# Dilated attention followed by soft MoE: a mask built by doubling, and the MoE expert stages and their PSUM banks in another order

## The chip, the cores and the metric

The kernel runs on one core of one Trainium2 chip. Such a core has TensorE (PE in the profile; its weight loads are listed apart as PEld), VectorE (DVE), ScalarE (ACT), GpSimd (POOL), SyncE (SP) and 16 DMA engines. The metric is the device time of one execution in microseconds (us); lower is better. Times are compared as medians over several executions.

## The reference, cut to what matters

The first half is causal sliding attention over 8 batches, 8 heads, 576 positions and head dimension 64. Heads 0 to 3 use a plain window of 32 keys; heads 4 to 7 a dilated one, every fourth key out of 128. The result, as 4608 tokens of 512 features, goes through a soft mixture of experts with 8 experts of 4 slots each.

```python
mask_plain = (rel >= 0) & (rel < window)                                   # window = 32
mask_dil = (rel >= 0) & (rel < window * dilation) & (rel % dilation == 0)  # dilation = 4
...
logits = x @ phi                                   # 4608 x 32
d = np.exp(logits - logits.max(0, keepdims=True))
d /= d.sum(0, keepdims=True) + 1e-09
slot_input = (d.T @ x).reshape(E, S_per_e, D)      # 8 experts, 4 slots, 512
for e in range(E):
    h = np.maximum(slot_input[e] @ w1[e], 0.0)     # 4 x 1024
    slot_out[e] = h @ w2[e]                        # 4 x 512
c = np.exp(logits - logits.max(1, keepdims=True))
c /= c.sum(1, keepdims=True) + 1e-09
return c @ slot_out.reshape(n_slots, D)            # 4608 x 512
```

## The kernel before

The program is written out by hand. Each `@blk.<engine>` block appends instructions to that engine's queue, and every engine works through its own queue in order. `WT` makes an engine wait for semaphore counts, `SIG` raises one. A `Slot` remembers who wrote a buffer (`ready`) and who read it (`reads`); `war()` is the list that a new writer has to wait for.

**Setup (L199 to L258).** POOL builds an identity matrix and an index ramp, and fetches `phi`. DVE clears the eight PSUM banks and builds four 0/1 mask tiles in bf16, two for the plain window and two for the dilated one. The dilated pattern is a 128 x 256 band: the identity is added 32 times into `mtmp2`, each time 4 columns further right (L246 to L250), and every addition waits for the one before. Five copies (L251 to L257) then fill `mask_dA` and `mask_dB`.

**Attention (L324 to L539).** There are 32 units, one for each batch and pair of heads, in a software pipeline: load (`st_dmas`), cast of q on DVE (`st_qcast`), transposes on PE, evacuation on ACT, scores, exponentials on ACT, masking on DVE, the product with V (`st_pv`), normalisation into `x_sb`. q comes through SP's queue, three units ahead at most; k and v come through POOL's queue with a cast from f32 to bf16 on the way, and with every fourth unit 1 MB of `w1` (bf16) comes too. The first cast of q stands behind the masks on DVE.

**Slot inputs (L629 to L742).** x is transposed in groups of four tiles, the logits are computed and exponentiated, transposed to `e_tok` (tokens by slots), and `e_tok` times x is accumulated in `psF`. L769 scales the sum by the column sums, four transposes and a copy (L779, L788) give `siT`.

**Experts (L793 to L890).** `m6_stageA(e)` multiplies `siT` by `w1` in two halves of four matmuls (L806), ACT applies relu to each half (L817), PE transposes the result in eight small pieces (L830), DVE copies them to `hT` (L840). `m6_stageB(e)` multiplies `hT` by `w2` in eight matmuls (L855), ACT copies the 4 x 512 result to `so4` (L870), PE transposes it in four pieces (L879). The loop emits A of one expert, then B of the expert before. `w2` lives in a ring of three buffers; B(e) also lets POOL issue the load for e+3 (L618). The banks: A uses `psA`, `psB` for even and `psC`, `psD` for odd experts, B uses `psE` and `psF` in turn, the transposes of A use `psG`, those of B `psH`.

**Combine weights (L895 to L950).** After the last expert, L895, L905 and L914 turn the slot outputs into `so_slots`. Then DVE sums `e_tok` over the slots, inverts and scales it (L921, L924, L926) to `c_tok`, and nine rounds of four PE transposes into `psG` (L939) and one DVE copy (L948) give `cT`.

**Output (L952 to L996).** 36 tiles of 128 x 512: one matmul each from `cT` and `so_slots` (L961) into six banks in turn, copied by ACT or DVE to one of six staging buffers (L972, L979), and written out by SP's, ACT's or POOL's queue (L988).

Of the kernel before, what the change touches and what calls it, by code (L numbers as in the profile page):

```python
# [6 lines left out]
AluOp = mybir.AluOpType  # L7
ACTF = mybir.ActivationFunctionType
F32 = mybir.dt.float32
BF16 = mybir.dt.bfloat16  # L10
# [4 lines left out]
E_EXP = 8  # L15
SLOTS_PER_E = 4
N_SLOTS = E_EXP * SLOTS_PER_E
FF = 1024
SCALE = 1.0 / (D ** 0.5)
N_TT = N_TOK // 128  # L20
# [90 lines left out]
def bass_dilated_sliding_attn__then__soft_moe_slots_kernel(  # L111
# [14 lines left out]
    WT = env.waits  # L126
    SIG = env.sig
# [6 lines left out]
    ident = A(nc.sbuf_tensor("ident", [128, 128], BF16))  # L134
# [3 lines left out]
    mask_dA = A(nc.sbuf_tensor("mask_dA", [128, 512], BF16))  # L138
    mask_dB = A(nc.sbuf_tensor("mask_dB", [128, 512], BF16))
# [11 lines left out]
    mtmp1 = AA(nc.sbuf_tensor("mtmp1", [128, 512], BF16))  # L151
    mtmp2 = AA(nc.sbuf_tensor("mtmp2", [128, 512], BF16))
# [23 lines left out]
    blk = A(nc.Block())  # L176
# [43 lines left out]
    @blk.vector  # L220
    def _(vv):
        ev = None
        for pb in ps_sc + ps_pv + [ps_ta, ps_tb]:
            ev = SIG(vv, vv.memset(pb[:], 0.0))
        for s_ in sl_sc + sl_pv + [sl_pta, sl_ptb2]:
            s_.written(ev)
        if _DBG_STAGE:
            SIG(vv, vv.memset(x_sb[:], 0.0))
        WT(vv, [ev_iota[0]])
        e2 = SIG(vv, vv.tensor_scalar(mtmp1[:, 0:192], mtmp0[:, 0:192], 287.0, None, op0=AluOp.is_le))  # L230
        e3 = SIG(vv, vv.tensor_scalar(mtmp2[:, 0:192], mtmp0[:, 0:192], 256.0, None, op0=AluOp.is_ge))
        WT(vv, [e2, e3])
        e4 = SIG(vv, vv.tensor_tensor(mtmp1[:, 0:192], mtmp1[:, 0:192], mtmp2[:, 0:192], AluOp.mult))
        e5 = SIG(vv, vv.memset(mask_plA[:], 0.0))
        e6 = SIG(vv, vv.memset(mask_plB[:], 0.0))
        WT(vv, [e4, e5, e6])
        SIG(vv, vv.tensor_copy(mask_plA[:, 0:160], mtmp1[:, 0:160]))
        SIG(vv, vv.tensor_copy(mask_plA[:, 256:416], mtmp1[:, 0:160]))
        SIG(vv, vv.tensor_copy(mask_plB[:, 0:160], mtmp1[:, 0:160]))
        SIG(vv, vv.tensor_copy(mask_plB[:, 256:416], mtmp1[:, 0:160]))  # L240
        evm = SIG(vv, vv.tensor_copy(mask_plB[0:64, 448:512], mtmp1[0:64, 0:64]))
        sl_mask_pl.written(evm)
        WT(vv, [evm] + sl_ident.ready)
        e8 = SIG(vv, vv.memset(mtmp2[:, 0:256], 0.0))
        WT(vv, [e8])
        for kk in range(32):  # L246
            ei = SIG(vv, vv.tensor_tensor(mtmp2[:, 4 * kk:4 * kk + 128],
                                          mtmp2[:, 4 * kk:4 * kk + 128],
                                          ident[:, :], AluOp.add))
            WT(vv, [ei])  # L250
        SIG(vv, vv.tensor_copy(mask_dA[:, 0:256], mtmp2[:, 0:256]))  # L251
        SIG(vv, vv.tensor_copy(mask_dA[:, 256:512], mtmp2[:, 0:256]))
        e13 = SIG(vv, vv.memset(mask_dB[:], 0.0))
        WT(vv, [e13])
        SIG(vv, vv.tensor_copy(mask_dB[:, 0:256], mtmp2[:, 0:256]))
        SIG(vv, vv.tensor_copy(mask_dB[:, 256:448], mtmp2[:, 0:192]))
        evm = SIG(vv, vv.tensor_copy(mask_dB[0:64, 448:512], mtmp2[0:64, 0:64]))  # L257
        sl_mask_dl.written(evm)  # L258

    units = [(b_, p_) for b_ in range(B) for p_ in range(4)]  # L260
# [303 lines left out]
    e_tok = MA(nc.sbuf_tensor("e_tok", [128, N_TT, N_SLOTS], BF16))  # L564
    c_tok = MA(nc.sbuf_tensor("c_tok", [128, N_TT, N_SLOTS], BF16))
# [16 lines left out]
    psA, psB, psC, psD = ps_sc  # L582
# [4 lines left out]
    sl_psG, sl_psH = sl_pta, sl_ptb2  # L587
    psA_bf = psA[:].bitcast(BF16)
    psB_bf = psB[:].bitcast(BF16)
    psD_bf = psD[:].bitcast(BF16)  # L590
    psE_bf = psE[:].bitcast(BF16)
    psF_bf = psF[:].bitcast(BF16)
# [197 lines left out]
        sl_psE.reads.append(ev)  # L790
        sl_siT.written(ev)

    hbank = [[(psA, sl_psA), (psB, sl_psB)], [(psC, sl_psC), (psD, sl_psD)]]  # L793
    sobank = [(psE, sl_psE), (psF, sl_psF)]

    def m6_stageA(e):
        ep = e % 2
        for hh in range(2):
            psX, slX = hbank[ep][hh]

            @blk.tensor
            def _(pe, e=e, hh=hh, psX=psX, slX=slX):
                WT(pe, sl_siT.ready + sl_w1.ready + slX.war())
                last = None
                for c in range(4):
                    last = pe.matmul(psX[0:SLOTS_PER_E, 0:512],  # L806
                                     siT[:, c, 4 * e:4 * e + 4],
                                     w1b[:, e, c, 512 * hh:512 * hh + 512],
                                     start=(c == 0), stop=(c == 3))
                ev = SIG(pe, last)  # L810
                slX.written(ev)
                sl_siT.reads.append(ev)

            @blk.scalar
            def _(ac, e=e, hh=hh, psX=psX, slX=slX, ep=ep):
                WT(ac, slX.ready + (sl_h[ep].war() if hh == 0 else []))
                ev = SIG(ac, ac.activation(h_sb[ep][0:SLOTS_PER_E, 512 * hh:512 * hh + 512],  # L817
                                           psX[0:SLOTS_PER_E, 0:512], ACTF.Relu))
                slX.reads.append(ev)
                if hh == 0:  # L820
                    sl_h[ep].written(ev)
                else:
                    sl_h[ep].ready.append(ev)

        @blk.tensor
        def _(pe, e=e, ep=ep):
            WT(pe, sl_h[ep].ready + sl_psG.war())
            last = None
            for cc in range(8):
                last = pe.transpose(psG_bf[:, 4 * cc:4 * cc + 4],  # L830
                                    h_sb[ep][0:SLOTS_PER_E, 128 * cc:128 * cc + 128],
                                    ident[0:SLOTS_PER_E, 0:SLOTS_PER_E])
            ev = SIG(pe, last)
            sl_psG.written(ev)
            sl_h[ep].reads.append(ev)

        @blk.vector
        def _(vv, e=e, ep=ep):
            WT(vv, sl_psG.ready + sl_hT[ep].war())
            ev = SIG(vv, vv.tensor_copy(hT[ep][:, :, :],  # L840
                                        psG_bf[:, 0:32].rearrange("p (c s) -> p c s", s=4)))
            sl_psG.reads.append(ev)
            sl_hT[ep].written(ev)

    def m6_stageB(e):
# [22 lines left out]
        def _(ac, e=e, psX=psX, slX=slX, ep=ep):  # L868
# [2 lines left out]
            slX.reads.append(ev)  # L871
            sl_so4[ep].written(ev)

        @blk.tensor
        def _(pe, e=e, ep=ep):
            WT(pe, sl_so4[ep].ready + sl_psH.war())
            last = None
            for fc in range(4):
                last = pe.transpose(psH_bf[:, 32 * fc + 4 * e:32 * fc + 4 * e + 4],  # L879
                                    so4[ep][0:SLOTS_PER_E, 128 * fc:128 * fc + 128],  # L880
                                    ident[0:SLOTS_PER_E, 0:SLOTS_PER_E])
            ev = SIG(pe, last)
            sl_so4[ep].reads.append(ev)
            sl_psH.ready = list(sl_psH.ready) + [ev]

    for step in range(E_EXP + 1):
        if step < E_EXP:
            m6_stageA(step)
        if 0 <= step - 1 < E_EXP:
            m6_stageB(step - 1)  # L890

    @blk.vector
    def _(vv):
# [18 lines left out]
    def _(vv):  # L912
# [1 line left out]
        ev = SIG(vv, vv.tensor_copy(so_slots[:, :], psE_bf[0:N_SLOTS, 0:512]))  # L914
        sl_psE.reads.append(ev)
        sl_sos.written(ev)

    @blk.vector
    def _(vv):
        WT(vv, sl_etok.ready)  # L920
        e1 = SIG(vv, vv.tensor_reduce(rsum_tok[:, :], e_tok[:, :, :],  # L921
                                      mybir.AxisListType.X, AluOp.add))
        WT(vv, [e1])
        e2 = SIG(vv, vv.reciprocal(rsum_tok[:, :], rsum_tok[:, :]))  # L924
        WT(vv, [e2])
        ev = SIG(vv, vv.tensor_tensor(c_tok[:, :, :], e_tok[:, :, :],  # L926
                                      rsum_tok[:, :].unsqueeze(2).to_broadcast([128, N_TT, N_SLOTS]),
                                      AluOp.mult))
        sl_etok.reads.append(ev)
        sl_ctok.written(ev)  # L930

    for r in range(N_TT // 4):
        @blk.tensor
        def _(pe, r=r):
            WT(pe, sl_ctok.ready + sl_psG.war())
            last = None
            for ti in range(4):
                t = 4 * r + ti
                last = pe.transpose(psG_bf[0:N_SLOTS, 128 * ti:128 * ti + 128],  # L939
                                    c_tok[:, t, :], ident[:, :])  # L940
            ev = SIG(pe, last)
            sl_psG.written(ev)
            sl_ctok.reads.append(ev)

        @blk.vector
        def _(vv, r=r):
            WT(vv, sl_psG.ready + sl_cT.war())
            ev = SIG(vv, vv.tensor_copy(cT[:, 512 * r:512 * r + 512], psG_bf[0:N_SLOTS, 0:512]))  # L948
            sl_psG.reads.append(ev)
            sl_cT.written(ev)  # L950

    obank = [(psA, sl_psA), (psB, sl_psB), (psC, sl_psC),  # L952
             (psD, sl_psD), (psE, sl_psE), (psF, sl_psF)]
# [82 lines left out]
```

## Time and profile before

Six executions took 309.57 to 311.54 us, with a median of 310.3. The profiled execution took 311.0 us, of which its span (first to last instruction) is 309.2 us.

| Stage, by us from the start of the span | length, us | PE busy, us | DVE busy, us | ACT busy, us | moved, GB/s |
|---|---|---|---|---|---|
| setup, 0 to 18 | 18.00 | 0.01 | 15.36 | 1.28 | 111 |
| attention while loads run, 18 to 169 | 151.00 | 107.88 | 115.02 | 94.78 | 170 |
| attention, its end, 169 to 183.5 | 14.50 | 11.75 | 13.76 | 7.20 | 3 |
| slot inputs, 183.5 to 217 | 33.50 | 30.71 | 11.18 | 15.84 | 95 |
| experts, 217 to 264.2 | 47.20 | 34.59 | 2.84 | 14.09 | 112 |
| combine weights, 264.2 to 277.4 | 13.20 | 5.51 | 6.72 | 0.00 | 0 |
| output, 277.4 to 309.2 | 31.80 | 16.87 | 11.89 | 9.99 | 298 |

A row of the profile's timeline gives start and length in us, the engine, the line of the source, the operation, the tile written and the tiles read, the stationary tile of a matmul as rows*columns, the shape, how many instructions are merged, and in square brackets how long the engine sat idle before and what released it. A row of the windows view gives busy time and number of instructions of each engine in a stretch, then the TensorE clock that was granted (1.00 is full speed), the DMA share and the rate. The end of a matmul is modelled: a series of eight that follow each other shows as 1.89 us, but the next matmul may start 1.83 us after the first.

### The profile page before, as it was taken

The numbers are of one execution on the slowest core, as the hardware profiler recorded it, in microseconds if no ns is written. First come the engines' busy times: TensorE is split into PE (matmuls) and PEld (weight loads), VectorE is DVE, ScalarE is ACT, GpSimd is POOL, SyncE is SP. The second block draws the span as 40 slices with busy tenths as digits, with TensorE's granted clock in tenths as the row PEclk, the third lists the DMA queues.
The fourth block names the chain that finished last, engine by engine and source line by source line (L and its number), as shares of the span: only waits on it lengthen the run. The fifth ranks groups of instructions, "written<-read, shape, count | busy, mean of one in ns | idle before, by whom it ended". The sixth has DMA issues, their size and how long they took to land.

```text
span 309.2 us, 6011 instructions
## 1 busy us (share of the span) xinstructions
PE 207.3 (67%) x2188; PEld 124.7 (40%) x2188; DVE 176.8 (57%) x480; ACT 143.2 (46%) x271; POOL 143.3 (46%) x204
## 2 busy tenths in 40 slices
PE   0047738689298594894776979998677777357660
PEld 0035426466176463673555655443223222132110
DVE  8865929969589787696895994222100000634441
ACT  1058717748378465484873716443323333003440
POOL 7999939779299595695980003000012110001221
PEclk9999999999999999999999999999999999755555
DMA  5899999999999999999999007950059993008796
GB/s 123 69 184 161 193 160 166 181 157 180 168 157 191 156 172 178 156 189 158 161 188 124 2 0 122 205 84 1 0 71 171 189 196 57 0 0 324 310 353 238
DMA packets 131197, 45.56 MB, mean 147 GB/s; under 512 B 115024, under 2 KB 123216, under 8 KB 131168
## 3 DMA queue, kind: packets, MB, share of 16 engines
q0 software_dynamic: 89824, 29.44, 82.4%
q1 hardware_dynamic: 39616, 12.59, 24.9%
q10 hardware_dynamic: 1728, 3.15, 2.7%
q8 instruction: 18, 0.29, 0.4%
q14 instruction: 11, 0.09, 0.1%
HBM read 61.93 MB, written 9.44 MB: 231 GB/s over the span
## 4 chain that ended last, share of the span: by engine, by line
DMA 35%; PE 32%; POOL 14%; DVE 8%; issue 5%; ACT 4%; ACTq 0%; POOLq 0%; DVEq 0%
DMA kb<-in_k_dram 32%; POOL vb L354 5%; PE ps_sc L806 5%; PE ps_pv L855 5%; POOL kb L347 4%; PE ps_pv L488 4%; DMA out_dram<-ostg 3%; PE ps_pv L727 3%; DVE x_sb L517 2%; PE ps_sc L645 2%; PE ps_ta L939 2%; POOL w1b L363 2%; PE ps_sc L677 2%; PE ps_sc L961 2%; POOL vb L357 2%
## 5 line engine op out<-in xcount | busy, mean ns | idle before, releaser
L441 ACT ACTIVATE pte<-ps_sc 128x512 bf16<-128x512 f32 (+1 forms) x128 | 65.9, 584 | 29.1 <-PE ps_sc L425 29.1
L347 POOL DMA_DIRECT2D kb<-in_k_dram x64 | 49.9, 798 | 27.1 <-PE ps_tb L390 26.7
L517 DVE TENSOR_TENSOR x_sb<-ps_pv,rinv 64x320 bf16<-64x320 f32 (+1 forms) x128 | 58.3, 456 | 4.2
L488 PE MATMUL ps_pv<-vb,pt 128*64 128x65 bf16 (+1 forms) x928 | 51.8, 249 | 2.5 <-DVE x_sb L517 2.5
L354 POOL DMA_DIRECT2D vb<-in_v_dram x64 | 49.4, 787 | 2.3 <-PE ps_sc L425 1.8
L390 PE MATMUL ps_tb<-ident,kb 96*128 96x96 bf16 x192 | 21.4, 279 | 38.0 <-DMA kb<-in_k_dram 37.8
L488 PEld LDWEIGHTS ps_pv<-vb,pt 128*64 128x64 bf16 (+1 forms) x928 | 40.8, 150 | 13.8 <-DVE x_sb L517 3.2
L618 POOL DMA_DIRECT2D w2r<-in_moe_w_dram x8 | 7.1, 885 | 80.8 <-PE ps_pv L855 56.9
L425 PE MATMUL ps_sc<-QT,KT 64*128 64x160 bf16 (+3 forms) x320 | 33.3, 342 | 5.3 <-ACT KT L404 4.0
L404 ACT ACTIVATE KT<-ps_tb 128x576 bf16<-128x576 bf16 x32 | 21.4, 669 | 27.9 <-PE ps_tb L390 27.7
L390 PE MATMUL ps_ta<-ident,qb 96*128 96x96 bf16 x192 | 21.1, 277 | 18.0 <-DVE qb L375 18.0
L390 PEld LDWEIGHTS ps_tb<-ident,kb 96*128 96x128 bf16 x192 | 15.5, 137 | 42.1 <-DMA kb<-in_k_dram 41.8
L988 POOL DMA_DIRECT2D out_dram<-ostg x12 | 6.5, 544 | 50.0 <-ACT ostg L972 44.2
L404 ACT ACTIVATE QT<-ps_ta 128x576 bf16<-128x576 bf16 x32 | 21.4, 669 | 16.6 <-PE ps_ta L390 16.6
L508 DVE RECIPROCAL rinv<-ps_pv 128x5 f32<-128x5 f32 x64 | 12.1, 188 | 25.3 <-PE ps_pv L488 24.4
L425 PEld LDWEIGHTS ps_sc<-QT,KT 64*128 64x128 bf16 (+1 forms) x320 | 17.4, 126 | 20.3 <-issue 9.7
L840 DVE COPY hT<-ps_ta 128x32 bf16<-128x32 bf16 x8 | 1.4, 175 | 38.2 <-PE ps_ta L830 38.2
L390 PEld LDWEIGHTS ps_ta<-ident,qb 96*128 96x128 bf16 x192 | 14.4, 132 | 19.9 <-issue 18.0
L357 POOL DMA_DIRECT2D vb<-in_v_dram x32 | 20.4, 637 | 0.0
L375 DVE CAST qb<-qs 96x768 bf16<-96x768 f32 x32 | 19.2, 601 | 0.3 <-DMA qs<-in_q_dram 0.3
L817 ACT ACTIVATE h_sb<-ps_sc 4x512 bf16<-4x512 f32 x16 | 9.4, 587 | 17.2 <-PE ps_sc L806 17.2
L806 PE MATMUL ps_sc<-w1b,siT 128*4 128x512 bf16 x64 | 15.1, 379 | 0.3 <-DVE siT L788 0.3
(97 smaller groups left out, 264.4 us busy)
## 6 DMA issues: line engine op xcount, KB each, us to landing
qs<-in_q_dram SPq DMA_DIRECT2D x64, 144.0 KB, 8.9
w1b<-in_moe_w_dram POOLq DMA_DIRECT2D x8, 1024.0 KB, 12.1
w2r<-in_moe_w_dram POOLq DMA_DIRECT2D x8, 1024.0 KB, 10.8
kb<-in_k_dram POOLq DMA_DIRECT2D x64, 72.0 KB, 12.3
vb<-in_v_dram POOLq DMA_DIRECT2D x64, 64.0 KB, 12.1
out_dram<-ostg SPq DMA_DIRECT2D x12, 256.0 KB, 2.9
out_dram<-ostg ACTq DMA_DIRECT2D x12, 256.0 KB, 3.2
out_dram<-ostg POOLq DMA_DIRECT2D x12, 256.0 KB, 2.8
```

Of the source, the lines that this page charges most:

```text
L347: ins = g.dma_start(kbs[:, :, 64 * hx:64 * hx + 64], k[b, h, 0:576, :].rearrange("(c p) d -> p c d", p=96))
L354: ins = g.dma_start(vbb[:, hx, 0:4, 0:D], v[b, h, 0:512, :].rearrange("(c p) d -> p c d", p=128))
L357: ins = g.dma_start(vbb[0:64, 0:2, 4, 0:D], v[b, h0:h0 + 2, 512:576, :].rearrange("h p d -> p h d"))
L375: ev = SIG(vv, vv.tensor_copy(qb[tpar][:, :, :], qs[slot][:, :, :]))
L390: last = pe.transpose(psX_bf[:, 96 * c:96 * c + 96], srcb[:, c, :], ident[0:96, 0:96])
L404: ev = SIG(ac, ac.activation(dst[:, :], psX_bf[:, 0:S], ACTF.Copy))
L425: inst = pe.matmul(o_ap, lhsT, rhs, start=True, stop=True)
L441: ev = SIG(ac, ac.activation(hc["pteb"][bi][:, 0:wc], hc["scb"][bi][:, 0:wc], ACTF.Exp, scale=SCALE))
L488: last = pe.matmul(o_ap, lhsT, rhs, start=(ji == 0), stop=(ji == len(js) - 1))
L517: evn = SIG(vv, vv.tensor_tensor(dst, src, rb, AluOp.mult))
L806: last = pe.matmul(psX[0:SLOTS_PER_E, 0:512], siT[:, c, 4 * e:4 * e + 4], w1b[:, e, c, 512 * hh:512 * hh + 512], start=(c == 0), stop=(c = ...
L855: last = pe.matmul(psX[0:SLOTS_PER_E, 0:DM], hT[ep][:, cc, :], w2r[ri][:, cc, :], start=(cc == 0), stop=(cc == 7))
```

## The change

Three things change, and the line numbers behind L245 shift.

**The dilated mask.** Two buffers are cleared and the identity is copied into one. Then five times the band so far is copied to the other buffer and added to itself with a shift of 4, 8, 16, 32 and 64 columns.

```diff
-        for kk in range(32):
-            ei = SIG(vv, vv.tensor_tensor(mtmp2[:, 4 * kk:4 * kk + 128],
...
+        ei = SIG(vv, vv.tensor_copy(mtmp2[:, 0:128], ident[:, :]))
+        WT(vv, [ei])
+        bufs = [mtmp2, mtmp1]
+        cur = 0
+        sh = 4
+        while sh <= 64:
+            src, dst = bufs[cur], bufs[1 - cur]
+            ei = SIG(vv, vv.tensor_copy(dst[:, 0:256], src[:, 0:256]))
+            WT(vv, [ei])
+            ei = SIG(vv, vv.tensor_tensor(dst[:, sh:256], dst[:, sh:256],
+                                          src[:, 0:256 - sh], AluOp.add))
+            WT(vv, [ei])
+            cur = 1 - cur
+            sh *= 2
```

**The combine weights ahead of the experts.** The DVE block of `c_tok` and the nine rounds of transposes and copies stand between `siT` and the first expert now, and use bank `psC` instead of `psG`.

```diff
-            WT(pe, sl_ctok.ready + sl_psG.war())
+            WT(pe, sl_ctok.ready + sl_psC.war())
...
-                last = pe.transpose(psG_bf[0:N_SLOTS, 128 * ti:128 * ti + 128],
+                last = pe.transpose(psC_bf[0:N_SLOTS, 128 * ti:128 * ti + 128],
                                     c_tok[:, t, :], ident[:, :])
```

**The expert stages.** The transposes of A with their copy become a stage C of their own, the transposes of B a stage D, and one step emits A(e), B(e-1), C(e), D(e-1). In every step the queue of PE held A(e), C(e), B(e-1), D(e-1) before. A uses `psD`, `psE` for odd experts, B uses `psF` alone.

```diff
-    hbank = [[(psA, sl_psA), (psB, sl_psB)], [(psC, sl_psC), (psD, sl_psD)]]
-    sobank = [(psE, sl_psE), (psF, sl_psF)]
+    hbank = [[(psA, sl_psA), (psB, sl_psB)], [(psD, sl_psD), (psE, sl_psE)]]
+    sobank = [(psF, sl_psF), (psF, sl_psF)]
...
     for step in range(E_EXP + 1):
         if step < E_EXP:
             m6_stageA(step)
         if 0 <= step - 1 < E_EXP:
             m6_stageB(step - 1)
+        if step < E_EXP:
+            m6_stageC(step)
+        if 0 <= step - 1 < E_EXP:
+            m6_stageD(step - 1)
```

## The prediction

> **What bounds the kernel now.** I read the windows by stage first, then the chain of waits, then PE's timeline stage by stage. Until about 168 us the chain waits for `kb` transfers, so loads bound the attention stage. From 183.5 us the chain is PE almost alone with short hops to ACT and DVE, until the output's transfers take over at about 280 us. So the change can pay only in the experts and the combine weights. The timeline, one expert step of the steady part:
>
> ```profile
> 226.67 1.89 PE L806 MATMUL ps_sc<-w1b,siT 128*4 128x512 bf16 x8
> ...
> 229.24 0.35 PE L830 MATMUL ps_ta<-ident,h_sb 4*128 4x4 bf16 x8 [0.68 <-ACT h_sb L817]
> ...
> 229.52 1.89 PE L855 MATMUL ps_pv<-w2r,hT 128*4 128x512 bf16 x8
> ...
> 232.09 0.25 PE L879 MATMUL ps_tb<-ident,so_1 4*128 4x4 bf16 x4 [0.68 <-ACT so_1 L870]
> ...
> 232.27 1.89 PE L806 MATMUL ps_sc<-w1b,siT 128*4 128x512 bf16 x8
> ```
>
> PE waits 0.68 us for ACT twice in each step; a step is 232.27 - 226.67 = 5.60 us. Then the combine weights, where PE and DVE take turns:
>
> ```profile
> 264.14 1.33 DVE L921 TENSOR_REDUCE rsum_tok<-e_tok 128x36 f32<-128x1152 bf16 x1
> 265.51 0.38 DVE L924 RECIPROCAL rsum_tok<-rsum_tok 128x36 f32<-128x36 f32 x1
> 265.92 1.36 DVE L926 TENSOR_TENSOR c_tok<-e_tok,rsum_tok 128x1152 bf16<-128x1152 bf16 x1
> 267.33 0.60 PE L939 MATMUL ps_ta<-ident,c_tok 128*32 128x128 bf16 x4 [3.57 <-DVE c_tok L926]
> ...
> 268.44 0.61 PE L939 MATMUL ps_ta<-ident,c_tok 128*32 128x128 bf16 x4 [0.51 <-DVE cT L948]
> ```
>
> PE stands still 3.57 us, then nine rounds follow, 1.115 us apart. The third thing is TensorE's clock. In the windows view of PE alone (busy, instructions, granted clock, DMA share, GB/s):
>
> ```profile
> 171.26:174.68 3.42, 3.42 (x48) 1.00 0.00 0
> ...
> 184.92:188.33 3.41, 3.41 (x25) 1.00 0.17 28
> 260.01:263.42 3.41, 2.37 (x17) 1.00 0.00 0
> 263.42:266.84 3.42, 0.34 (x4) 1.00 0.00 0
> 266.84:270.25 3.41, 1.82 (x12) 0.50 0.00 0
> ...
> 280.49:283.90 3.41, 3.41 (x10) 0.50 0.96 364
> ```
>
> The clock falls to half at 266.84, in the idle time ahead of L939. It is also low before 188.3 us, though the row says 1.00 there; the durations tell:
>
> ```profile
> 185.18 1.06 PE L645 MATMUL ps_sc<-ident,x_sb 128*128 128x128 bf16 x8
> ...
> 188.62 0.62 PE L645 MATMUL ps_sc<-ident,x_sb 128*128 128x128 bf16 x8
> ```
>
> The same eight transposes take 1.06 us before and 0.62 us after. So the trace has one rise (188.33) and one fall (266.84), 78.51 us or 23.0 stretches of 3.413 us apart.
>
> **The mask.** 32 dependent additions from 7.75 to 16.20 us (0.26 us each), with the memset ahead 8.6 us, go. In come two memsets and a copy (0.17 and 0.20 us, rows of L244 and L237), and five pairs of a 256-wide copy and an addition of 192 to 252 columns: 5 x (0.27 + 0.32), from L251 and L456 (0.39 us at 448 wide) with the wait. That is about 3.5 us, so the masks are ready about 5 us sooner, and the first casts and q loads of units 3 and 4 with them. I count it as 0: the end of this stage is set by `kb` transfers, whose queue is filled by POOL from 8.48 us on whatever DVE does; moved q loads only take their share of the DMA engines earlier. Bounds: -1.5 us if those loads fill the 10 to 14 us stretch, where rates are still below 105 GB/s; +1 us if DVE's copies, now beside POOL's first loads, slow these as they did one pair of `kb` issues (2.27 us beside copies at 16.36, 1.50 us at 8.48).
>
> **The combine weights, moved.** Nothing is taken out. Old place: from `so_slots` (264.21) to the first L961 (277.36), 13.15 us, gone there but for the 0.1 us from DVE to PE. New place: DVE comes to it after `siT` (218.18), and all PE work of the experts is queued behind its transposes. 1.33 + 0.38 + 1.36 and gaps make 3.2 us; eight rounds of 1.115 and a last 0.45 (stage A waits for no copy) make 9.4. Sum 12.6 us for 13.05: **-0.45 us**. The nine copies are queued before the first `hT` copy on DVE and done by then; no DMA is moved past anything but the `w2` issues on POOL, which wait for B either way. The new bank psC was last read by ACT long before. All this is at half clock; at full clock a round loses 4 x (107 - 56) ns (from 1.06 and 0.62 us above, less the drain), 1.8 us for nine.
>
> **The stage order.** New step: A 1.83 (start to start), B begins at once (its `hT` is a step old, `psF` was read a step ago), C at 1.83 after B's start, its relu then over 1 us old; D waits for `so4`, 2.57 us after B's start as now (232.09 - 229.52); D to A 0.18. 1.83 + 2.57 + 0.18 = 4.58 us for 5.60. C's wait goes behind B, and C fills 0.28 of D's wait. Seven steps have both A and B: 7 x 1.01 = **-7.1 us**. The first A and last B keep their waits. Late next is `w2`: the DMA rows show at most 207 GB/s in this stage, so 5.1 us per 1 MB, more than 4.58. But from B(0)'s end, five loads are in after about 29 us (the last is issued at 18.8, and they take 9.2 to 10.8 us to land), and B(7) starts at 30.2. It is hidden by 1 us; 0 to +2.
>
> **The clock.** The moved wait stands before the experts now. PE's last long matmuls there end at 216.74; then come four tiny transposes, and nothing until L939 at 221.4, 4.7 us. A stretch of 3.41 us with 0.34 us busy lost the clock, and however such stretches are laid over this gap, one has under 12% of array time (rounds at full clock fill 24%). I take the fall as near certain. Then the rounds cost 1.115 as now, and the experts begin at half clock: matmuls of 427 ns (1.71 us for four in the chain, L961) for 229 ns.
>
> When does it rise? The Trainium skill, TensorE: Matmul & The Clock Gate, Part 1, says that about 3.4 us of sustained activity releases the clock and one idle window of that length takes it; the trace has the length. But being busy isn't enough here: 171.26 and 280.49 above are busy throughout and stay slow. Their stationary tiles have 64 and 96 rows among them, or 32; the stretch before the rise ran 128 rows all the time. Part 4 says that transposes don't count as busy. Here they did: 184.92 to 187.02 was L645 transposes alone, then 1.3 us of L677. By the page matmuls alone would count, and 1.3 us of them in a stretch would do: A(0) alone would raise the clock, a loss of about 2.5 us. By the rows I need one whole stretch of 128-row streaming. A(0) is 3.4 us long, too short unless aligned; A(1) and B(0) together are 6.83 us without a gap, which always holds one. On average the clock rises 5.1 us into that pair: 3.4 + 5.1 = 8.5 us at half speed, that is **+4.25 us** (3.4 to 5.1). I take the rows.
>
> **Output.** L961 begins at full clock: about -0.3 us to the first write; the rest is bound by transfers (about 400 GB/s).
>
> **Sum** on the span 309.2: 0 - 0.45 - 7.1 + 4.25 - 0.3 = -3.6, so 305.6. The profiled execution took 311.0, 1.8 above its span and 0.7 above the median of 310.3; -3.6 on the median is **306.7 us**, 304.5 to 308.5 by this case's own bounds.
>
> **Rivals.**
> - *The clock does not fall* (0.12). For it: one stretch with 0.34 us busy is the only fall seen, and the limit could be below what the gap leaves. Then -0.45 - 1.8 - 7.1 - 0.3 = -9.65: 300.6 us.
> - *The clock falls and never rises in the experts* (0.14), the case on the other side. For it: L806 and L855 use 4 of 128 columns, and no slow stretch in the trace shows whether such matmuls raise the clock; that they kept it up does not tell. A cold step is 3.41 + 3.41 + 0.74 + 0.25 = 7.8 us. A(0) +1.6, seven steps of +3.2, B(7) +1.6: +25.6 for +4.25, 328 us. It decides from the third pair on: with A(0) and two cold steps the 7.85 us of gain are gone.
> - *It rises late* (0.10), if two full stretches in a row are needed: 2 to 3 cold steps, 308.5 to 314 us.
> - *`w2` binds or the mask costs* (0.04): up to +3, about 309.5.
> - The forecast has 0.60.
>
> Differences over 0.3% (0.9 us) can be told from no change by this measurement. Faster 0.70 (forecast, no fall), same 0.06, slower 0.24 (no rise, most of late rise). The range from 299.5 to 311.5 leaves out no rise and part of late rise.
>
> **What would show it.** Mask additions end near 11 us, and the `kb` wait still ends near 165. L939's work starts near 221 and the granted clock is 0.50 by 225. L806 begins near 231 with 427 ns pitch and turns to 229 ns in the second step. Steps of 4.6 us, no wait of PE on ACT before C, 0.4 us before D. If L806 keeps 427 ns to the last expert, the sum is wrong by its largest term; if B waits for `w2`, by the `w2` margin.

## The result, and the profile after

The changed kernel takes 307.91 us (median of 5, 306.17 to 308.57), the kernel before 310.83 (median of 10). The ratio is 0.9896, with a 95% interval of 0.9863 to 0.9929: faster by about 1%, clear of noise. On the median, 306.7 us was forecast. The profiled execution has a span of 305.4 us for 309.2, and forecast was 305.6. The total agrees better than its parts do. Measured from the starts of the same instructions in both timelines:

| Piece | before, us | after, us | difference |
|---|---|---|---|
| start to transposes of the slot inputs (L779, now L791) | 217.65 | 218.22 | +0.57 |
| from there to A(0) | 0.58 | 12.74 | +12.16 |
| A(0) to D(7) | 44.57 | 41.59 | -2.98 |
| D(7) to the first output matmul | 14.56 | 1.69 | -12.87 |
| first output matmul to the end | 31.84 | 31.18 | -0.66 |
| sum | 309.20 | 305.42 | -3.78 |

PE's timeline of the changed kernel, beginning and end of the experts:

```profile
221.86 0.40 PE L826 MATMUL ps_sc<-ident,c_tok 128*32 128x128 bf16 x4 [3.38 <-DVE c_tok L813]
222.76 0.61 PE L826 MATMUL ps_sc<-ident,c_tok 128*32 128x128 bf16 x4 [0.51 <-DVE cT L835]
...
230.96 2.88 PE L852 MATMUL ps_sc<-w1b,siT 128*4 128x512 bf16 x8
234.51 0.35 PE L879 MATMUL ps_ta<-ident,h_sb 4*128 4x4 bf16 x8 [0.68 <-ACT h_sb L863]
...
236.51 1.89 PE L904 MATMUL ps_pv<-w2r,hT 128*4 128x512 bf16 x8
238.34 0.35 PE L879 MATMUL ps_ta<-ident,h_sb 4*128 4x4 bf16 x8
239.09 0.25 PE L931 MATMUL ps_tb<-ident,so_0 4*128 4x4 bf16 x4 [0.40 <-ACT so_0 L919]
239.26 1.89 PE L852 MATMUL ps_sc<-w1b,siT 128*4 128x512 bf16 x8
...
264.34 1.89 PE L904 MATMUL ps_pv<-w2r,hT 128*4 128x512 bf16 x8 [0.43 <-issue]
266.16 0.35 PE L879 MATMUL ps_ta<-ident,h_sb 4*128 4x4 bf16 x8
266.91 0.25 PE L931 MATMUL ps_tb<-ident,so_0 4*128 4x4 bf16 x4 [0.40 <-ACT so_0 L919]
269.36 2.51 PE L904 MATMUL ps_pv<-w2r,hT 128*4 128x512 bf16 x8 [2.20 <-issue]
272.55 0.26 PE L931 MATMUL ps_tb<-ident,so_1 4*128 4x4 bf16 x4 [0.68 <-ACT so_1 L919]
```

Three things are to be seen. The step is as planned: C (L879, 238.34) has lost its wait, D (L931) waits 0.40 us instead of 0.68. A(0) takes 2.88 us, so the clock did fall, but rose again within it: eight matmuls at half clock would take 3.6 us. And B (L904) stands still ahead of the last experts, 2.20 us before B(7), with "issue" as the releaser: the profile names no engine that it waited for. The trace does have the landing of each `w2` load, though: those of experts 5, 6 and 7 land at 259.19, 264.25 and 269.27 us, and B(5), B(6) and B(7) each start 0.09 us later. In the kernel before, the last load landed at 258.68 us, 1.56 us ahead of B(7). The clock, in PE's windows (busy, instructions, granted clock, DMA share, GB/s):

```profile
215.87:219.28 3.41, 1.70 (x11) 1.00 0.00 0
219.28:222.70 3.42, 0.40 (x4) 1.00 0.00 0
222.70:226.11 3.41, 1.83 (x13) 0.50 0.00 0
...
229.52:232.94 3.42, 2.92 (x13) 0.50 0.02 5
232.94:236.35 3.41, 2.73 (x20) 1.00 0.00 0
...
267.07:270.48 3.41, 1.21 (x10) 1.00 0.44 72
270.48:273.90 3.42, 2.26 (x12) 0.50 0.00 0
```

It falls at 222.70, behind the stretch that holds the wait for `c_tok` and the first round, as forecast. It rises at 232.94 after 10.24 us (three stretches of 3.413), and falls again at 270.48, behind the stretch with the wait ahead of B(7).

### The profile page after: what moved, and what is told of

Its sections match the earlier page's. It is cut to its first block, busy times and chain, and to the rows that moved or that the text cites. A ratio compares the mean times of both kernels' runs of the same rounds, so it can differ in the third digit from the quotient of the medians.

```text
span 305.4 us, 5998 instructions
## 1 busy us (share of the span) xinstructions
PE 208.5 (68%) x2188; PEld 125.3 (41%) x2188; DVE 172.5 (56%) x460; ACT 143.5 (47%) x271; POOL 143.3 (47%) x204
## 4 chain that ended last, share of the span: by engine, by line
DMA 41%; PE 30%; POOL 12%; DVE 7%; issue 5%; ACT 3%; ACTq 0%; POOLq 0%; DVEq 0%
DMA kb<-in_k_dram 35%; DMA out_dram<-ostg 5%; PE ps_pv L904 5%; PE ps_sc L852 4%; POOL vb L365 4%; PE ps_pv L499 4%; PE ps_pv L739 3%; POOL kb L358 3%; POOL w1b L374 2%; DVE x_sb L528 2%; PE ps_sc L657 2%; PE ps_sc L826 2%; PE ps_tb L401 2%; PE ps_sc L689 2%; PE ps_sc L436 2%
## 5 line engine op out<-in xcount | busy, mean ns | idle before, releaser
L863 ACT ACTIVATE h_sb<-ps_sc 4x512 bf16<-4x512 f32 x12 | 7.0, 587 | 29.2 <-PE ps_sc L852 29.2
L467 DVE TENSOR_TENSOR pt<-pte,mask_plA 128x448 bf16<-128x448 bf16 x32 | 12.3, 384 | 11.9 <-ACT pte L452 11.6
```

The source lines that it names most:

```text
L467: ev = SIG(vv, vv.tensor_tensor(hc["ptb"][bi][:, 0:wc], hc["pteb"][bi][:, 0:wc], mk[:, 0:wc], AluOp.mult))
```

## The experiments

Below, **array time** of a stretch is worked out from the trace: for each matmul its moving columns at the clock of the moment, times the used rows over 128, summed and divided by 3.413 us. Two matmuls that run side by side in the two halves of the array's columns count once; the products with V do so in the attention, where they start in pairs 2 to 7 ns apart. Ratios are to the kernel before on the same chip, with 95% intervals.

### Each part alone

**The mask.** The kernel before with the new mask code of the diff and nothing else.

```diff
-        for kk in range(32):
-            ei = SIG(vv, vv.tensor_tensor(mtmp2[:, 4 * kk:4 * kk + 128],
...
+        while sh <= 64:
+            src, dst = bufs[cur], bufs[1 - cur]
```

> The doubled mask alone, everything else as before. Forecast: no change, since kb transfers set the end of this stage (within -1.5 and +1 us). Rival, from the changed kernel's trace, where the slot inputs start their last x product 0.57 us later than before: q loads that start 5 us sooner share the DMA engines with the first k and v loads, and the kernel is about 0.6 us slower. In the profile both want the first transposes of q at about 13.0 us; the forecast wants the start of the slot inputs at 183.5 +- 0.3, the rival at 184.1 or later.

310.61 us, ratio 0.9993 (0.9974 to 1.0012). PE's timeline, where the first transposes came at 17.99 us and L645 at 183.50 us before:

```profile
12.95 0.64 PE L401 MATMUL ps_ta<-ident,qb 96*128 96x96 bf16 x6 [12.95 <-DVE qb L386]
...
183.60 1.03 PE L656 MATMUL ps_sc<-ident,x_sb 128*128 128x128 bf16 x8
```

DVE and PE begin 5.0 us sooner, and the slot inputs start where they did. The last long `kb` transfer of the chain ends where it did, too (165.21 us for 165.10). The forecast holds, with its reason. The 0.57 us of the first row of the table isn't the mask's doing: in the profiled executions of this study that run the attention, these first transposes start anywhere from 183.5 to 185.8 us, with the old mask as with the new.

**The stage order.** The kernel before with stages C and D, the step order and the banks, and nothing else.

```diff
         if 0 <= step - 1 < E_EXP:
             m6_stageB(step - 1)
+        if step < E_EXP:
+            m6_stageC(step)
+        if 0 <= step - 1 < E_EXP:
+            m6_stageD(step - 1)
```

> The stage order and banks alone; mask as before, combine weights behind the experts as before. Forecast: seven steps of 4.6 us for 5.6 us, w2 hidden, -7.1 us. Rival: B waits for w2 in the last steps, because the last step has no stage A in front of B(7), so B(7) is due 28 us after B(0)'s end and its load lands after 30.6 us (both from the changed kernel's trace): -7.1 + 3.3 = about -3.8 us, and the clock falls at the end as before or one stretch earlier.

308.05 us, ratio 0.9915 (0.9889 to 0.9942), that is -2.6 us, and -3.4 to -1.8 by the interval. The last two B of its timeline:

```profile
252.73 1.89 PE L859 MATMUL ps_pv<-w2r,hT 128*4 128x512 bf16 x8 [1.45 <-issue]
...
257.78 1.89 PE L859 MATMUL ps_pv<-w2r,hT 128*4 128x512 bf16 x8 [2.23 <-issue]
```

A(0) to D(7) is 219.47 to 260.34, 40.87 us for 44.57: -3.7, what the rival gave. The whole kernel gained less: the rival's -3.8 lies outside the interval. In this execution the slot inputs started late (185.83 us for 183.50); whether that is so in all of them is not shown. Half of the stage order's gain is missing with the other two parts away, so it isn't these that took it.

**The combine weights ahead.** The kernel before with the DVE block and the nine rounds moved and in `psC`.

```diff
+        sl_ctok.written(ev)
+
+    for r in range(N_TT // 4):
+        @blk.tensor
+        def _(pe, r=r):
+            WT(pe, sl_ctok.ready + sl_psC.war())
...
     hbank = [[(psA, sl_psA), (psB, sl_psB)], [(psC, sl_psC), (psD, sl_psD)]]
...
-            WT(pe, sl_ctok.ready + sl_psG.war())
```

> The combine weights ahead of the experts alone; mask and stage order as before. Forecast: the clock falls before the experts and rises only after a whole stretch of 128-row streaming: -0.45 + 4.25 = +3.8 us; without stage order A(0) and A(1) are 3.4 us each with a wait between them, so the rise could come even later. Rival: a stretch that is filled to about 0.8 raises the clock, as in the changed kernel, where the rise came 2 us into A(0): the loss is 1 to 2 us, the sum +0.5 to +1.5 us.

310.85 us, ratio 1.0019 (0.9992 to 1.0047): no gain, a loss of 1.5 us at most. The clock falls and rises as in the changed kernel. In PE's windows:

```profile
216.99:220.40 3.41, 1.77 (x11) 1.00 0.00 0
220.40:223.82 3.42, 0.40 (x4) 1.00 0.00 0
230.64:234.06 3.42, 2.92 (x13) 0.50 0.02 5
234.06:237.47 3.41, 2.73 (x20) 1.00 0.00 0
```

The rise came behind a stretch with two rounds of transposes and 1.9 us of A(0) in it, 0.81 of array time. A whole stretch of streaming isn't needed. In this run B(7) waits as well, for a moment, and here the profile names the load:

```profile
275.36 1.89 PE L890 MATMUL ps_pv<-w2r,hT 128*4 128x512 bf16 x8 [0.22 <-DMA w2r<-in_moe_w_dram]
```

### The wait ahead of B

**`w2` loaded into the dead `xT`.** In the changed kernel, once the logits are done (L689), nobody reads `xT` again. Experts 3 to 6 get their `w2` there, at once, and not when B(0) to B(3) free a buffer.

```diff
+    w2t = [w2r[i][:, :, :] for i in range(3)] + [
+        xT_flat[:, 4096 * i:4096 * i + 4096].rearrange("p (c f) -> p c f", f=DM) for i in range(4)]
...
+    @blk.gpsimd
+    def _(g):
+        WT(g, xT_reads)
+        for e in range(3, 7):
+            issue_w2(g, e)
```

> The changed kernel with w2 of experts 3 to 6 loaded into the dead xT buffer as soon as the logits are done, instead of waiting for B(0) to B(3). Forecast as recorded (w2 hidden): no change against the changed kernel, 307.9. Rival (w2 binds): the 3.3 us of waits ahead of B(5), B(6) and B(7) go, and with the 2.2 us wait ahead of B(7) the fall of the clock in it (0.6 us in B(7)): about -3.9 us against the changed kernel, 304.0.

303.93 us, ratio 0.9784 (0.975 to 0.9818). The changed kernel had 0.9896: 3.5 us less by the ratios, 4.0 by the medians, and 37.63 us for 41.59 from A(0) to D(7). The waits are gone, and B(7) is at full clock:

```profile
263.45 1.89 PE L915 MATMUL ps_pv<-xT,hT 128*4 128x512 bf16 x8
...
266.20 1.89 PE L915 MATMUL ps_pv<-w2r,hT 128*4 128x512 bf16 x8
268.76 0.25 PE L942 MATMUL ps_tb<-ident,so 4*128 4x4 bf16 x4 [0.68 <-ACT so L930]
```

"issue" in the profile of the changed kernel was the wait for `w2`: the landings say so, and so does this run, in which only the place and time of the loads differ.

**The same with the stage order alone.** The kernel before with the stage order and banks, and `w2` in `xT` as above.

```diff
+        if step < E_EXP:
+            m6_stageC(step)
+        if 0 <= step - 1 < E_EXP:
+            m6_stageD(step - 1)
...
+        WT(g, xT_reads)
+        for e in range(3, 7):
+            issue_w2(g, e)
```

> The kernel before with the stage order and banks and with w2 in the dead xT buffer; mask and combine weights as before. If w2's waits took about half of what the stage order is worth, the forecast's own term comes back here: seven steps of 4.48 for 5.60 us, 7.8 us off the experts, and in the profile 36.7 us from A(0) to D(7) instead of 44.6. The median is 303 +- 1. Rival, that the stage order is worth only what it showed alone: 308.

303.32 us, ratio 0.9738 (0.9708 to 0.9767). In its timeline:

```profile
218.41 1.89 PE L818 MATMUL ps_sc<-w1b,siT 128*4 128x512 bf16 x8 [0.32 <-DVE siT L800]
...
255.13 0.25 PE L897 MATMUL ps_tb<-ident,so 4*128 4x4 bf16 x4 [0.68 <-ACT so L885]
```

36.72 us for 44.57. With `w2` there in time the stage order is worth 7.85 us, a little more than forecast. This kernel, without the moved combine weights and the new mask, is no slower than the one with them (0.9738 for 0.9784, with intervals that just overlap).

### The clock

**Keeping it up.** In the changed kernel, 14 matmuls without use ahead of the rounds, and one behind each.

```diff
+    def fill(n):
+        @blk.tensor
+        def _(pe):
+            WT(pe, sl_phi.ready + sl_psD.war())
+            last = None
+            for kf in range(n):
+                last = pe.matmul(psD[0:N_SLOTS, 0:512], phi_sb[:, kf % 4, :], x_sb[:, kf % 4, :],
+                                 start=True, stop=True)
...
+    fill(14)
```

> The changed kernel, with 14 matmuls of 128 rows by 512 columns into the unused bank psD put on PE ahead of the rounds of combine weights, and one such matmul behind each round; their results are not used. Reading of the traces so far: a stretch of 3.41 us under about 0.36 of 128-row array time loses the clock. Every stretch has 0.45 or more now, so the clock stays up until the end of the experts: a round takes 0.91 instead of 1.115 us and A(0) 1.85 instead of 2.88, together about -2.6 us against the changed kernel, with the waits for w2 ahead of B(5) to B(7) as they were: 305.3. Rival, that the clock cost little because it would have to be paid elsewhere (w2 waits grow by what is won): 307.9, no change.

304.26 us, ratio 0.9773 (0.9741 to 0.9805). By the timeline a round takes 0.90 us and A(0) runs at full clock; but the wait ahead of B(7) is still there and costs the clock, which was expected to stay up to the end of the experts:

```profile
222.59 0.40 PE L839 MATMUL ps_sc<-ident,c_tok 128*32 128x128 bf16 x4 [0.29 <-DVE cT L850]
...
229.34 1.89 PE L867 MATMUL ps_sc<-w1b,siT 128*4 128x512 bf16 x8
...
267.51 3.57 PE L919 MATMUL ps_pv<-w2r,hT 128*4 128x512 bf16 x8 [2.23 <-issue]
```

```profile
266.48:269.89 3.41, 2.38 (x6) 0.50 0.03 7
```

From the slot inputs to the end of A(0), 2.5 us are won (1.45 up to A(0), 1.0 in it). Of these, 1.9 us are given back behind it: the waits for `w2` add up to 4.0 us for 3.25, and B(7) takes 3.57 us for 2.51. That the waits grew because of the clock is not shown: they came to 4.15 us with the stage order alone, too. By the ratios the gain over the changed kernel is 3.8 us, more than the 2.6 expected. The profiled execution, the slowest of six, shows 1.7 us of it, and each ratio is open by about 1 us; where the rest comes from stays open. The windows row shows 2.38 us of B(7), about 0.70 of array time, in a stretch behind which the clock did not rise.

**Both together.** The two edits above in one kernel.

> The filling matmuls and w2 in the dead xT buffer together. If the two costs are separate they add up: -2.6 and -4.0 against the changed kernel's 307.9, about 301.3. If w2's waits were in part made by the clock or the other way round, less.

298.21 us, ratio 0.9598 (0.9569 to 0.9628), 3 us better than expected. B(7) starts without a wait and at full clock:

```profile
262.84 1.89 PE L930 MATMUL ps_pv<-w2r,hT 128*4 128x512 bf16 x8
```

Adding what each took off the ratio gives 0.966, about 2 us short, though four intervals of about 1 us stand in that sum. The timelines show the same: from the slot inputs to D(7), `w2` in `xT` wins 3.75 us over the changed kernel, the filling matmuls 0.6, and both together 6.3. The 1.9 us between are what the filling matmuls alone gave back, by the longer waits for `w2` and the half-speed B(7). So the two costs are not separate: the wait ahead of B(7) takes the clock with it.

**What raises and keeps it.** Attention and MoE are left out and the output is zeros; PE runs series of matmuls.

```diff
...
+    seq = [[(128, 4, 32)], [(96, 128, 32)], [(64, 128, 32)], [(32, 128, 32)], [(128, 128, 32)],
+           [(128, 4, 48), (64, 128, 40)], [(128, 4, 48), (32, 128, 40)], [(128, 4, 32)]]
+    for grp in seq:
+        idle(10)
+        for (r_, c_, n_) in grp:
+            run_pe(r_, c_, n_)
```

> Attention and MoE are left out, the output is zeros; PE runs series of matmuls with 512 columns moving, 10 us of idling ahead of each: 32 with 128 rows and 4 columns of weights, 32 with 96 rows, 32 with 64, 32 with 32, 32 with 128 (all with 128 columns), then 48 of 128 x 4 followed by 40 of 64 rows, 48 of 128 x 4 followed by 40 of 32 rows. If the clock goes by rows times time: 128 x 4 and 128 x 128 raise it after one to two stretches of 3.41 us, 64 and 32 rows never do, 96 rows (0.75) lies between what has raised it so far (0.79) and what has not (0.66); after a rise 64 rows (0.5) keep it, 32 rows (0.25) lose it within two stretches. If it goes by being busy: every series raises and keeps it. If it goes by rows times columns: 128 x 4 never raises it.

Stretches of PE's windows, one or two of each of the first four series, then of 64 and of 32 rows after a rise:

```profile
32.09:35.51 3.42, 3.42 (x10) 1.00 0.00 0
35.51:38.92 3.41, 3.41 (x17) 1.00 0.00 0
...
52.57:55.99 3.42, 3.42 (x9) 0.50 0.00 0
73.05:76.47 3.42, 3.42 (x9) 0.50 0.00 0
76.47:79.88 3.41, 3.41 (x10) 0.50 0.02 5
...
103.77:107.19 3.42, 3.42 (x9) 0.50 0.00 0
158.39:161.80 3.41, 3.41 (x17) 1.00 0.00 0
...
192.52:195.93 3.41, 3.41 (x18) 1.00 0.00 0
195.93:199.35 3.42, 3.42 (x10) 0.50 0.00 0
```

All are busy throughout; the number of matmuls of 512 columns tells the clock (9 or 10 at half, 17 or 18 at full; the first line has 10 and is slow, though the row gives 1.00 ahead of the first record). With 128 rows and 4 columns the clock rises behind the first full stretch; with 128 x 128 it does so behind a stretch that was not quite full. With 96 rows it rises behind the one of 52.57. With 64 and 32 rows it never rises in their four stretches. After a rise 64 rows keep it, 32 lose it behind one full stretch. So it goes by rows times time; the columns of the weights do not count, and being busy is not enough.

### A version that beats both

With `w2` in `xT`, the sums and reciprocals of the combine weights go ahead of L769 on DVE, the scaling behind `siT`, and one round of transposes into each expert step, where PE waits.

```diff
+        WT(vv, sl_etok.ready)
+        e1 = SIG(vv, vv.tensor_reduce(rsum_tok[:, :], e_tok[:, :, :],
...
+        if step == 0:
+            c_round(0)
         if step < E_EXP:
             m6_stageC(step)
+        if step > 0:
+            c_round(step)
         if 0 <= step - 1 < E_EXP:
             m6_stageD(step - 1)
```

> The changed kernel with w2 in the dead xT buffer, the sums and reciprocals of the combine weights on DVE ahead of the scaling of the slot inputs (while PE still runs the x product), c_tok behind siT, and one round of transposes in each expert step, in PE's wait between C and D. Expected from the timelines: the 12.7 us between the transposes of the slot inputs and A(0) shrink to 0.6, A(0) runs at full clock (-1.0), the rounds hide in waits of 0.4 us (0.22 us each at full clock): -13.2 us against the w2 kernel's 303.9, about 291. Rival: DVE gets late, so that the slot inputs start 1 us later and hT waits for copies of cT: about 294.

289.53 us, ratio 0.9308 (0.9283 to 0.9334), 6% under the changed kernel and a little better than expected. One step of its timeline:

```profile
218.83 1.89 PE L862 MATMUL ps_sc<-w1b,siT 128*4 128x512 bf16 x8 [0.32 <-DVE siT L816]
...
221.67 1.02 PE L862 MATMUL ps_sc<-w1b,siT 128*4 128x512 bf16 x4
...
225.22 0.35 PE L889 MATMUL ps_ta<-ident,h_sb 4*128 4x4 bf16 x8
225.50 0.40 PE L836 MATMUL ps_sc<-ident,c_tok 128*32 128x128 bf16 x4
225.97 0.25 PE L941 MATMUL ps_tb<-ident,so 4*128 4x4 bf16 x4
226.15 1.89 PE L862 MATMUL ps_sc<-w1b,siT 128*4 128x512 bf16 x8
```

A(0) starts 0.58 us behind the slot inputs, a step takes the same 4.48 us with a round in it (221.67 to 226.15), and D no longer waits. The clock stays up into the output (it falls at 260.33, the first output matmul is at 257.01). The rival's late DVE isn't seen.

## Why the prediction was right, and where it was not

The total was right (-3.6 us on the span forecast, -3.8 found), but two terms of it were wrong by 3 to 4 us each, in opposite directions: `w2` and the clock. That they cancel is luck; neither had to do with the other in the forecast.

- **The mask, 0.** Right, for the reason given: alone it moves the first transposes by 5 us, and the last `kb` transfer and the slot inputs by 0.1 us.
- **The combine weights, -0.45.** About right: 12.16 us added and 12.87 saved, -0.7 (the first round still ran at full clock, 0.90 us). In the new place PE waits for them as long as in the old, so that moving them gained nothing; hiding them did, in the last experiment.
- **The stage order, -7.1.** Right as a term: -7.85 us with `w2` in time. A and B overlap a little more than counted, so a step is 4.48 us, not 4.58.
- **`w2`, "B(7) starts at 30.2. It is hidden by 1 us; 0 to +2".** This step failed. It counts seven full steps from B(0)'s end to B(7), but the last step has no A in front of B, 1.83 us less: by its own numbers B(7) is due at 28.4 and the load lands at 29. In the changed kernel B(7) would be due 27.8 us after B(0)'s end (six steps of 4.48 and 2.75, less 1.83), and starts 31.0 us after it (269.36 less 238.34). The waits are 0.4, 0.6 and 2.3 us, together +3.25 us, and the clock that falls behind them makes B(7) another 0.6 us longer. The landing was wrong, too. The forecast let the last load take 9.2 to 10.8 us from its issue, but 10.8 is the median of the kernel before. And the loads follow each other: they are issued 4.3 to 4.7 us apart and land 5.0 to 5.8 us apart, so each is later than the one before. The last took 12.7 us and landed 30.9 us after B(0)'s end, not 29. So the step that failed is the due time of B(7), and with it the landing; the waits are the term of 0 that should have been 3.9 us with the clock.
- **The clock, "I need one whole stretch of 128-row streaming. A(0) is 3.4 us long, too short unless aligned".** The fall was forecast right, and that rows count and columns don't. The size of what is needed was wrong: 0.75 (the probe) to 0.81 (this kernel, 229.52) of a stretch is enough, so the last rounds and the first 2 us of A(0) raised it. The term was +4.25 us, and +2.5 by the page's rule as the prediction read it; A(0) lost 1.0 us. The Trainium skill's page TensorE: Matmul & The Clock Gate (Part 1) has the length of the stretch right, but its rule, that sustained activity releases the clock, is too wide here: 64 rows without a gap for four stretches did not. Its Part 4 says that in transpose mode the full clock does not engage, because such work doesn't count as busy in the same way. The profile does not tell whether these transposes run in that mode, but they counted: the stretch from 184.92 in the kernel before raised the clock with only 1.3 us of other matmuls, 0.38 of array time, and up to 0.70 was not enough.
- **The output, -0.3.** It came to -0.66 us, but not for the reason given: the clock had fallen ahead of it again. Over the executions profiled, this stretch takes 30.2 to 32.0 us where the clock is at half from its start or soon after, so -0.66 is within the scatter; its cause was not tried.

So A(0) to D(7): -7.85 + 3.25 + 0.6 + 1.0 = -3.0 us, the -2.98 of the table. In the rivals, "`w2` binds" had 0.04, and a price of up to +3, and was what happened; the case of a clock that never rises is out, by the probe too, since four columns of weights raise it like 128.

## What to carry to other kernels

Where a stage is made faster, count the due time of every transfer that it waits for again, last step included; half of this change's best part was given back to a prefetch that was just in time before. A wait that is moved costs the same in its new place unless something fills it. Serial work on a slow side path, like these nine rounds, pays when it is cut up and put into waits that are there anyway.

## What the runs showed of the hardware

- The TensorE clock is decided in stretches of 3.413 us that run on from its first change (all rises and falls in one trace are whole numbers of them apart). Array time of 0.37 (the changed kernel, 215.87) and 0.39 (the combine weights alone, 216.99) kept it; 0.35 (with `w2` in `xT`, 215.91), 0.33 (the changed kernel, 267.07) and 0.25 (the probe) lost it. To rise it takes more: 0.50 and 0.60 (both in the probe) and about 0.70 (the filling matmuls, 266.48) were not enough, 0.75 (the probe) was. This hangs on counting side-by-side matmuls once: counted so, the attention of the kernel before has at most 0.67 in a stretch (181.50), and the clock did not rise; counted singly, that stretch would have 0.92.
- The granted clock is shown as 1.00 ahead of its first record, where durations give half speed: nine or ten matmuls of 512 columns in a stretch instead of 17.
- A wait for a DMA can show as "issue" in the profile; that it was `w2` came out from the landings in the trace, 0.09 us ahead of each B, and from the run where the load was moved.
